# Three norms of a fp32 transformer block turned on VectorE through DRAM, a new opening, and an order by forward and backward passes

## The chip, the cores and the metric

The kernel runs on one core of a Trainium2 chip. The metric is device time in microseconds (us). Matmuls and PE transposes run on TensorE (PE, with its weight loads shown as PEld), elementwise work on VectorE (DVE) and ScalarE (ACT), a few memsets on GpSimd (POOL). SyncE (SP) only issues DMAs; they run on 16 DMA engines shared by all queues. Each engine takes its instructions in a fixed order and waits at the first one whose inputs are not there.

## The reference

A pre-norm block on x of 2048 rows by 640 columns in fp32: windowed attention (32 heads of 20, a window of 8 keys two rows apart), then a SwiGLU feed-forward of 1728. The norms have no weights.

```python
def _layernorm(x, eps=1e-5):
    return (x - mean(x)) / sqrt(var(x) + eps)

qkv = _layernorm(x) @ wqkv                 # 640 x 1920
idx = pos[:, None] - arange(8) * 2         # negative ones are masked
o = softmax(q . k[idx] * Dh**-0.5) . v[idx]
h = x + o @ wo                             # 640 x 640
n = _layernorm(h)
out = h + (silu(n @ w_gate) * (n @ w_up)) @ w_down
```

## The kernel before, in words

The 2048 rows are four blocks (`NB`, called blocks 0 to 3 here, numbered b) of 512; a block is four row groups j of 128 rows (`NJ`). Columns go in five chunks of 128 (`NC`), heads in four groups g of 8 (`NG`), the feed-forward in 13 tiles of 128 columns and a last one of 64 (`NF`).

**Products in three passes.** Every fp32 operand of a product is split into a high half, rounded to PE's fp32r type by an ACT cast, and a low half, the rest, made by a DVE subtraction. A product is hi·hi + lo·hi + hi·lo in three PE passes. So each operand costs PE nothing before its product, but ACT a cast and DVE a subtraction.

**PE's work.** The qkv products are L415: 15 matmuls of 480 columns for a (b, g, j), 64 such groups. The output product of attention is L586, 480 matmuls of 320 columns. Gate and up are L649, three passes of five matmuls for each of two banks (5 and 6), 1620 in all; down is L665, into banks 0 to 4, 820 in all. Before qkv and before gate/up the normed rows have to stand turned, columns on partitions. In `x_columns`, five groups of four 128x128 PE transposes (L316, `to_columns`) turn a block into a bank; ACT casts it (L319) and DVE subtracts (L320). Block 0's first norm is turned in the opening row group by row group (L376, casts L378, subtractions L379). `warm` (L331) issues matmuls on zeros ahead of the first data. `finish` turns the fifth 128 columns of the down product back (L707), adds on DVE (L714, L718) and stores (L722).

**The norms.** `LnStats.one` is the ACT form: a pass that sums the rows (L258, an Identity whose output nobody needs), the negated mean (L259), for ln1 a pass that centres (L261) and one that squares and sums (L266). `one_dve` does the same with BN statistics on DVE (L276 to L278); in the opening row groups j = 0, 1, 2 use it and j = 3 uses ACT. `rstd` has a square root on ACT and a Newton step on DVE (L289 to L293); `apply` (L306) scales. For ln2 of block 3 alone (`TURN = (3,)`), `apply` writes the rows in columns of 32 instead, DVE transposes 32x32 pieces of the whole tile (L738), four DMAs write it to the scratch `xsc` in DRAM (L740), one reads it back turned (L744), and ACT and DVE split it into shb (L733, L734). No PE transposes are needed there.

**Loads.** x of block 0 is loaded by row groups (L348), qkv weights a chunk at a time (L388, cast L389, subtraction L391), five chunks for a head group. A constant of 160 columns holds the attention mask and the identity matrix that the PE transposes use (L751). Tiles of feed-forward weights come by L623, are cast by L624 and L625 and split by L641; block 0 stores the low halves to the scratch `lsc`, and blocks 1 and 2 read them back (L629) instead of computing them. Attention goes through DRAM scratch as well; its DVE products are L463 and L468 (q·k) and L494 to L502 (weights times v, one multiply for each row group, then a tree of adds).

**The order.** The program records operations with an engine, a cost, the tiles they read and write, and a priority. `Plan.order` runs a list scheduler over them, whose start times set the order on every engine and in the queue of SP; semaphores follow from reads and writes. So any change of operations or costs moves the order elsewhere too.

Of the kernel before, what the change touches and what calls it, by code (L numbers as in the profile page):

```python
# [1 line left out]

# [8 lines left out]
F32 = mybir.dt.float32  # L11
# [12 lines left out]
NF = 14  # L24
KEPT = range(NF)
LOADED = (1, 2)
TURN = (3,)
# [8 lines left out]
class Plan:  # L36

# [20 lines left out]
    def order(self):  # L60
# [57 lines left out]
        self.end = max(free.values())  # L118
        self.start = start
        return sorted(range(len(ops)), key=lambda n: (start[n], n))  # L120
# [17 lines left out]
def program(tc, x_in, wqkv_in, wo_in, ffn_in, ffl_in, const_in, out):  # L138
# [4 lines left out]
    FA_N = 16320 + 128 + 640 + 2688  # L143
    RA_N = 19200

    with tc.tile_pool(name="sb", bufs=1) as sb, tc.tile_pool(
# [26 lines left out]

        banks = [psp.tile([128, 512], F32, name=f"bank{i}") for i in range(8)]
# [5 lines left out]
        xsc = dr.tile([NB, D, 4, 128], F32, name="xsc")  # L180
        lsc = dr.tile([NF, 128, 1920], F32, name="lsc")

# [7 lines left out]
        KV = carve(3 * 1760)  # L190
        QT = carve(2 * 640)
        PROD = carve(2560)
        OG = carve(640)
        XN = carve(4 * 640)
        LG = carve(2 * 256)
        MX = carve(2 * 64)
# [22 lines left out]

        ident = f(IDENT, 128)  # L220
# [4 lines left out]
        P.add("DVE", 0.8, lambda: V.memset(f(PROD, 1120), 0.0), w=[rf(PROD, 1120)], prio=0)  # L225

        def zero_halo(t):
            Q.dma_start(
                t[:, :, 0 : W - 1, :].rearrange("g a r c -> (g a) (r c)"),
                fa[0 : NG * 2, PROD : PROD + 1120],  # L230
            )

        for nm, t in (("K", ksc), ("V", vsc)):
            P.add(
                "SP", 0.07, lambda t=t: zero_halo(t), r=[rf(PROD, 1120)],
# [4 lines left out]
        class LnStats:  # L240
# [11 lines left out]
            def one(self, j):  # L252
                src, xo = self.src, XN + 640 * j
                SUM, NEG, SS = self.SUM + j, self.NEG + j, self.SS + j
                junk = (lambda: act_t()[:, 3072:3712]) if self.turned else (lambda: f(xo, 640))

                def s1():
                    A.activation(junk(), src(j), AF.Identity, accum_out=f(SUM, 1))  # L258
                    A.mul(f(NEG, 1), f(SUM, 1), -1.0 / D)  # L259
                    if self.center:  # L260
# [3 lines left out]
                P.add("ACT", 1.95 if self.center else 2.15, s1, r=[self.srcr(j)], w=[("ab", 3072, 3712) if self.turned else rf(xo, 640), rf(SUM, 1), rf(NEG, 1)] + ([] if self.center else [rf(SS, 1)]), prio=self.prio)  # L264
                if self.center:
                    P.add("ACT", 1.0, lambda: A.activation(src(j), f(xo, 640), AF.Square, accum_out=f(SS, 1)),  # L266
                          r=[rf(xo, 640)], w=[self.srcr(j), rf(SS, 1)], prio=self.prio + 1)
# [13 lines left out]
            def rstd(self, j, n, after=()):  # L281
                STD, RS, TM, NEG, NB = (o + j for o in (self.STD, self.RS, self.TM, self.NEG, self.NB))
                var, vr, sc = f(self.SS + j, n), rf(self.SS + j, n), 1.0 / D
                if j in self.ondve:
                    var, vr, sc = f(MV + 2 * j + 1, 1), rf(MV + 2 * j, 2), 1.0
# [42 lines left out]
        def warm(n, after=()):  # L328
            def mm():
                for _ in range(n):  # L330
                    T.matmul(banks[4][:, 0:128], r_(WARM, 128), r_(WARM, 128), start=True, stop=True)  # L331
# [509 lines left out]
```

## Time and profile before

| | |
|---|---|
| median of 3 runs | 865.08 us (864.16 to 865.6) |
| span of the profiled execution | 863.4 us |
| PE transposes of norms, L316 | 120, 16.7 us busy |
| PE transposes of block 0's first norm, L376 | 20, 4.1 us |
| warm-up matmuls, L331 | 23, 5.4 us |
| DVE statistics, L276 | 6, 2.6 us |
| turning on DVE, L738 | 1, 2.8 us |
| PE clock granted | 1.00 in every stretch asked |

The span counts from the first to the last instruction of one execution; the time of a run has about 1.7 us (865.08 - 863.4) around it. "Busy" of PE counts a matmul until its last column has drained, so consecutive matmuls overlap: the step from one to the next, which a long chain row gives, is what a matmul costs, and not its mean duration. A row of the timeline shows start, duration of the whole run, engine, line, operation, count, and in brackets how long the engine was idle before it and who released it.

### The profile page before, as it was taken

To read this page: it belongs to the slowest core of one execution; us is meant where nothing else is said; L and a number is where in the kernel's file an instruction comes from. 1 tells how busy PE (TensorE), PEld (TensorE's weight loads), DVE (VectorE), ACT (ScalarE), POOL (GpSimd) and SP (SyncE) were. 2 spreads that over 40 slices of the span, in tenths; PEclk is the share of its full clock that TensorE was granted. 3 is DMA by queue.
4 is the path that set the end of the run, shared out by engine and by line. 5 is a ranking of instruction groups with operands and counts; after the bars stand their busy time and mean duration, and the time that the engine had idled before them with its cause. 6 is when DMAs were issued, how large, how long until landed. Compare 5 with 4: busy or idle time off the path is not lost.

```text
span 863.4 us, 10743 instructions
## 1 busy us (share of the span) xinstructions
PE 857.4 (99%) x4059; PEld 731.0 (85%) x4059; DVE 645.4 (75%) x743; ACT 402.4 (47%) x651; POOL 1.8 (0%) x8
## 2 busy tenths in 40 slices
PE   9999999999999999999999999999999999999998
PEld 8888888889888888988888898888898887888886
DVE  7499999999989999988989898999622226333332
ACT  6867743233753435564434457443447324332321
POOL 0000000000000000000000000000000000000000
PEclk9999999999999999999999999999999999999999
DMA  7997766497597978568997985897733755222301
GB/s 266 269 295 215 177 173 173 141 285 189 168 332 237 292 243 302 139 182 277 344 276 243 321 238 165 256 340 226 251 122 117 248 185 197 92 92 92 102 21 61
DMA packets 74611, 180.10 MB, mean 209 GB/s; under 512 B 28720, under 2 KB 39344, under 8 KB 73792
## 3 DMA queue, kind: packets, MB, share of 16 engines
q1 hardware_dynamic: 74560, 179.43, 66.7%
q8 instruction: 31, 0.51, 0.2%
q14 instruction: 20, 0.16, 0.1%
HBM read 138.36 MB, written 41.03 MB: 208 GB/s over the span
## 4 chain that ended last, share of the span: by engine, by line
PE 98%; DVE 1%; DMA 1%; ACT 0%; SPq 0%; issue 0%; DVEq 0%; ACTq 0%
PE bank L649 42%; PE bank L415 24%; PE bank L665 21%; PE bank L586 8%; PE bank L316 2%; DMA fa<-in_x_dram 1%; PE bank L376 0%; PE bank L707 0%; DVE ra L641 0%; ACT ra L624 0%; DVE fa L276 0%; DVE acts L694 0%; DVE fa L692 0%; DVE shb L734 0%; DVE fa L278 0%
## 5 line engine op out<-in xcount | busy, mean ns | idle before, releaser
L649 PE MATMUL bank<-shb,ra 128*128 128x512 f32 x1620 | 378.9, 389 | 0.0
L649 PEld LDWEIGHTS bank<-shb,ra 128*128 128x128 f32 x1620 | 303.3, 188 | 62.2 <-ACT fa L683 0.2
L665 PE MATMUL bank<-ra,acts 128*128 128x512 f32 x656 | 160.5, 391 | 0.0
L665 PEld LDWEIGHTS bank<-ra,acts 128*128 128x128 f32 x656 | 122.4, 188 | 25.1
L684 DVE TENSOR_TENSOR fa<-bank,fa 128x512 f32<-128x512 f32 x52 | 35.9, 690 | 119.0 <-PE bank L649 118.8
L415 PE MATMUL bank<-ra,sha 128*128 128x480 f32 x480 | 107.6, 383 | 0.0
L415 PE MATMUL bank<-ra,shb 128*128 128x480 f32 x470 | 104.9, 380 | 0.0
L415 PEld LDWEIGHTS bank<-ra,sha 128*128 128x128 f32 x480 | 90.7, 190 | 13.5
L415 PEld LDWEIGHTS bank<-ra,shb 128*128 128x128 f32 x470 | 87.4, 188 | 12.8
L624 ACT CAST ra<-fa 128x1280 fp32r<-128x1280 f32 (+1 forms) x56 | 68.8, 1228 | 62.5 <-PE bank L649 60.4
L494 DVE TENSOR_TENSOR fa<-fa 128x1280 f32<-128x1280 f32 x64 | 93.1, 1486 | 0.8
L502 DVE TENSOR_TENSOR fa<-fa 128x1280 f32<-128x1280 f32 (+2 forms) x96 | 89.8, 935 | 2.8
L463 DVE TENSOR_TENSOR fa<-fa 128x2560 f32<-128x2560 f32 x32 | 90.3, 2820 | 1.4 <-DMA fa<-qsc 1.0
L468 DVE TENSOR_REDUCE fa<-fa 128x128 f32<-128x2560 f32 x32 | 90.1, 2816 | 0.7
L683 ACT ACTIVATE fa<-bank 128x512 f32<-128x512 f32 x52 | 31.1, 599 | 108.5 <-PE bank L649 108.4
L641 DVE TENSOR_TENSOR ra<-fa,ra 128x640 fp32r<-128x640 f32 (+1 forms) x82 | 64.8, 818 | 17.5 <-ACT ra L625 15.0
L586 PE MATMUL bank<-ra 128*128 128x320 f32 x480 | 74.5, 309 | 0.0
L586 PEld LDWEIGHTS bank<-ra 128*128 128x128 f32 x480 | 72.4, 188 | 2.1
L420 ACT ACTIVATE st<-bank,fa 128x480 f32<-128x480 f32 x64 | 42.1, 661 | 68.4 <-PE bank L415 59.1
L625 ACT CAST ra<-fa 128x640 fp32r<-128x640 f32 x56 | 40.7, 729 | 64.7 <-PE bank L665 64.6
L685 ACT CAST acts<-fa 128x512 fp32r<-128x512 f32 x52 | 32.2, 619 | 41.0 <-DVE fa L684 40.9
L665 PE MATMUL bank<-acts,ra 128*128 128x512 f32 x164 | 46.4, 391 | 0.6 <-DVE acts L694 0.6
(85 smaller groups left out, 497.4 us busy)
## 6 DMA issues: line engine op xcount, KB each, us to landing
fa<-in_ffn_dram SPq DMA_DIRECT2D x52, 960.0 KB, 6.1
ra<-lsc SPq DMA_DIRECT2D x26, 640.0 KB, 5.6
fa<-ksc SPq DMA_DIRECT2D x32, 440.0 KB, 5.8
fa<-vsc SPq DMA_DIRECT2D x32, 440.0 KB, 6.7
ra<-lsc SPq DMA_DIRECT2D x30, 320.0 KB, 3.2
lsc<-ra SPq DMA_DIRECT2D x13, 640.0 KB, 6.4
ksc<-st SPq DMA_DIRECT2D x32, 160.0 KB, 3.7
qsc<-st SPq DMA_DIRECT2D x16, 320.0 KB, 3.5
```

Source lines behind the costliest of these rows:

```text
L415: T.matmul(banks[bk][:, 0:480], l, r_(wq(g, w, c), 480), start=(p, c) == first_mm, stop=(p, c) == last_mm)
L420: P.add("ACT", act(480) + 0.06, lambda bk=bk, j=j: A.activation(stage_t()[:, so : so + 1920].rearrange("p (t j c) -> p t j c", t=3, j=NJ)[ ...
L463: P.add("DVE", dve(2560), lambda: V.tensor_tensor(f(PROD, 2560).rearrange("p (j w c) -> p j w c", j=2, w=W), window(ko, 2 * jp), f(qo + 32 ...
L468: P.add("DVE", dve(2560), lambda: V.tensor_reduce(f(lo + 128 * jp, 128), f(PROD, 2560).rearrange("p (n d) -> p n d", d=DH), axis=AX.X, op= ...
L494: V.tensor_tensor(f(PROD + 1280 * jj, 1280).rearrange("p (w h d) -> p w h d", w=W, d=DH), f(vo + 160 * j, 1280).rearrange("p (w h d) -> p ...
L502: V.tensor_add(dst(v), v[:, :, 0:m, :], v[:, :, m : 2 * m, :])
L586: T.matmul(banks[bk][:, 0:320], l, r_(m, 320), start=p == 0 and c == 0, stop=p == 2 and c == NC - 1)
L624: P.add("ACT", act(n), lambda: A.copy(r_(gu, n), f(raw, n)), r=[rf(raw, n)], w=[rr(gu, n)], prio=PR["fh"])
L625: P.add("ACT", act(640), lambda: A.copy(r_(dn[0], 640), f(raw + n, 640)), r=[rf(raw + n, 640)], w=[rr(dn[0], 640)], prio=PR["fh"])
L641: P.add(eng, c, lambda o=o: E.tensor_sub(ra[p0:, lo + o : lo + o + 640], fa[p0:, raw + o : raw + o + 640], ra[p0:, hi + o : hi + o + 640]. ...
L649: T.matmul(banks[bk], r_(gu + 1280 * w + wid * c + col, 128), x2(a, c), start=p == 0 and c == 0, stop=p == 2 and c == NC - 1)
L665: T.matmul(banks[k], l, m, start=first and p == 0, stop=last and p == len(passes) - 1)
```

## The change

**Turned norms.** `TURN = (3,)` becomes `TURN1, TURN2 = (2,), (2, 3)`. Ln1 and ln2 of block 2 now also go the way of block 3's ln2. `ln2_turn` becomes `turn` with a second scratch `ysc`, and `turned_columns` serves both. In the turned ln1 the summing pass writes the output that nobody needs onto its own source rows, and the centred rows go to `XN` in columns of 32. Wherever ln2 is not turned (block 1 now too), `rstd` and `apply` take three row groups first, then the last one; turned ones take all four at once.

**The opening.** Warm-up goes from 20 matmuls of 128 columns to 10 of 512, and from 3 between the first row groups to one of 512. The identity is made on GpSimd, and only the mask is loaded, later. SP issues x0, weights chunk 0, x1, chunks 1 and 2, chunks 3 and 4, x2, x3; before it was x0, the constant, x1, the five chunks, x2 and x3. Later weights also come two chunks to a DMA. Row groups j = 2 and 3 take ACT statistics, and `rstd` takes two groups at once.

**Attention.** K, V, q and products have tiles of their own, and the two multiplies by v of 1280 columns become one of 2560 (64 instructions become 32).

**The order.** The list scheduler (`listed`) gives start times; then all operations are placed from the end backwards and from the start forwards by modelled durations and latencies, twice; then 35 seeded moves (`MOVES`) shift some start times at random and repeat the passes. The final sequence is the sort by start.

```diff
-TURN = (3,)
+TURN1, TURN2 = (2,), (2,3)
...
+MOVES = [
+    (1000023, 3, 0.01), (1000040, 3, 0.01), (1000200, 3, 0.05), (1000252, 3, 0.01), (1001109, 3, 0.01), (1001162, 1, 0.05), (1001237, 1, 0.05), (1001256, 1, 0.01),
...
+    def forward(self, key):
+        st, lanes = [0.0] * len(self.ops), {}
+        for n in self.sort(key):
+            t = max([st[d] + self.dur[d] + self.gap(d, n) for d in self.pred[n]], default=0.0)
+            st[n] = lanes.setdefault(self.ops[n][0], Lane()).early(t, self.dur[n])
+        return st
+
+    def backward(self, st):
+        ends = [s + d for s, d in zip(st, self.dur)]
...
+    def move(self, st, seed, spread, share):
+        r = random.Random(seed)
+        key = [s + (r.gauss(0, spread) if r.random() < share else 0.0) for s in st]
+        return self.forward(self.backward(self.forward(key)))
+
+    def order(self):
+        st = self.listed()
+        self.model()
+        for _ in range(2):
+            st = self.forward(self.backward(st))
+        for m in MOVES:
+            st = self.move(st, *m)
+        return self.sort(st)
...
-                junk = (lambda: act_t()[:, 3072:3712]) if self.turned else (lambda: f(xo, 640))
+                away = self.turned and not self.center
+                junk = (lambda: act_t()[:, 3072:3712]) if away else (lambda: src(j)) if self.turned else (lambda: f(xo, 640))
...
-                    if self.center:
+                    if self.center and self.turned:
+                        A.activation(f(XN, 2560).rearrange("p (f j t) -> p f j t", j=NJ, t=32)[:, :, j, :], src(j).rearrange("p (f t) -> p f t", t=32), AF.Identity, bias=f(NEG, 1))
+                    elif self.center:
...
-        def warm(n, after=()):
+        def warm(n, wide, after=()):
...
+        def turned_columns(t, nm, prio):
...
+            src = lambda k: f(XN + 512 * k, 512).rearrange("p (q j t) -> p j q t", q=4, j=NJ)
...
+            for k in range(NC):
+                col = lambda a, k=k: t()[:, 2560 * a : 2560 * a + 2560].rearrange("p (j c q t) -> p c j q t", j=NJ, c=NC, q=4)[:, k]
+                P.add("ACT", act(512), lambda col=col, k=k: A.copy(col(0), src(k)), r=[rf(XN + 512 * k, 512)], w=hiv(k), prio=prio)
+                P.add("DVE", dve(512), lambda col=col, k=k: V.tensor_sub(col(1), src(k), col(0).bitcast(F32)),
+                      r=[rf(XN + 512 * k, 512), *hiv(k)], w=lov(k), prio=prio)
+
+        def turn(nm, dst, prio, first=False):
+            P.add("DVE", dve(2560), lambda: V.transpose(f(XN, 2560), f(XN, 2560)), r=[rf(XN, 2560)], w=[rf(XN, 2560)], prio=prio)
+            for q in range(4):
+                P.add("SP", 0.65, lambda q=q: Q.dma_start(
...
+            P.add("SP", 0.65, lambda: Q.dma_start(f(XN, 2560).rearrange("p (k t) -> p k t", k=NC), dst.rearrange("(k c) q t -> c k (q t)", c=128)),
...
+                if b in TURN1:
+                    turn(f"Y{b}", ysc[b], PR["ln1"], True)
+                    turned_columns(t, nm, PR["t1"])
+                    return
...
-                    warm(3, [("b5", 0, 0.25)])
-                (st.one_dve if j < 3 else st.one)(j)
+                    warm(1, 512, [("b5", 0, 0.25)])
+                (st.one_dve if j < 2 else st.one)(j)
...
-            for j in range(NJ):
-                st.rstd(j, 1, [(nm, 3200 + 1280 * (j // 2), 3840 + 1280 * (j // 2))])
...
+            for j in (0, 2):
+                st.rstd(j, 2, [(nm, 3200 + 640 * j, 3840 + 640 * j)])
+
+        def load_wqkv(g, parts=((0, 1), (2, 3), (4,))):
+            for ks in parts:
...
-                if b == 0 and j >= NJ - 2:
+                if b not in TURN2 and j >= NJ - 2:
...
-            if b:
+            if b in TURN2:
...
-        warm(20)
-        P.add("SP", 0.45, lambda: Q.dma_start(f(MASK, 160), const_in), w=[rf(MASK, 160)], prio=0, nbytes=nb(128, 640))
+        warm(10, 512)
+
+        def eye():
+            G.memset(ident, 1.0)
+            G.affine_select(ident, ident, pattern=[[-1, 128]], compare_op=ALU.is_equal, fill=0.0, base=0, channel_multiplier=1)
+        P.add("POOL", 1.2, eye, w=[rf(IDENT, 128)], prio=0)
+        load_wqkv(0, ((0,),))
         load_x(0, (1,))
-        load_wqkv(0)
+        load_wqkv(0, ((1, 2), (3, 4)))
         load_x(0, (2, 3))
```

**Where the order moves.** In these rows a name ahead of the arrow is what is written. In the change L810 is gate/up, L826 down, L868 the turning back in `finish`, L575 qkv, L444 the PE transposes of norms, L549 the casts of qkv weights, L532 the casts of block 0's turned rows, and L382, L383, L387 are the sum, the negated mean and the centring on ACT.

First place: ACT in the opening, before,

```order
L389 CAST ra_66<-fa_65 128x480
L378 CAST sha_133<-bank7_75 128x512
L378 CAST sha_133<-bank5_73 128x128
L389 CAST ra_66<-fa_65 128x480
L378 CAST sha_133<-bank6_74 128x512
L378 CAST sha_133<-bank5_73 128x128
L389 CAST ra_66<-fa_65 128x480 x3
L296 ACTIVATE fa_65<-fa_65 128x1 x2
L258 ACTIVATE fa_65<-fa_65 128x640
L259 ACTIVATE fa_65<-fa_65 128x1
L261 ACTIVATE fa_65<-fa_65 128x640
```

and in the change:

```order
L532 CAST sha_122<-bank5_73 128x128
L532 CAST sha_122<-bank7_75 128x512
L549 CAST ra_66<-fa_65 128x480 x2
L532 CAST sha_122<-bank6_74 128x512
L549 CAST ra_66<-fa_65 128x480 x2
L382 ACTIVATE fa_65<-fa_65 128x640
L383 ACTIVATE fa_65<-fa_65 128x1
L387 ACTIVATE fa_65<-fa_65 128x640
L382 ACTIVATE fa_65<-fa_65 128x640
L383 ACTIVATE fa_65<-fa_65 128x1
L387 ACTIVATE fa_65<-fa_65 128x640
L532 CAST sha_122<-bank5_73 128x128
```

The cast of the second row group's last chunk (bank 5) moves from ahead of the centring passes to behind both of them.

Second place: PE at the first feed-forward tile of block 0 (banks 5 and 6 of L649, then L810), before,

```order
L316 MATMUL bank6_74<-fa_65 128x128 x4
L316 MATMUL bank5_73<-fa_65 128x128 x4
L316 MATMUL bank7_75<-fa_65 128x128 x4
L415 MATMUL bank2_70<-ra_66,shb_67 128x480 x15
L316 MATMUL bank6_74<-fa_65 128x128 x4
L415 MATMUL bank3_71<-ra_66 128x480 x5
L415 MATMUL bank3_71<-ra_66,shb_67 128x480 x5
L415 MATMUL bank3_71<-ra_66 128x480 x5
L649 MATMUL bank5_73<-shb_67,ra_66 128x512 x5
L649 MATMUL bank6_74<-shb_67,ra_66 128x512 x5
```

and in the change:

```order
L444 MATMUL bank6_74<-fa_65 128x128 x4
L444 MATMUL bank5_73<-fa_65 128x128 x4
L444 MATMUL bank7_75<-fa_65 128x128 x4
L575 MATMUL bank3_71<-ra_66 128x480 x5
L575 MATMUL bank3_71<-ra_66,shb_67 128x480 x5
L575 MATMUL bank3_71<-ra_66 128x480 x5
L444 MATMUL bank6_74<-fa_65 128x128 x4
L810 MATMUL bank5_73<-shb_67,ra_66 128x512 x5
L810 MATMUL bank6_74<-shb_67,ra_66 128x512 x5
```

The last group of transposes moves from ahead of the last 15 qkv matmuls to directly ahead of gate/up, which reads what it turns.

Third place: the end on PE (down products into banks 0 to 4), before,

```order
L665 MATMUL bank4_72<-acts_2090,ra_66 128x512 x5
L665 MATMUL bank0_68<-ra_66,acts_2090 128x512 x5
L707 MATMUL bank4_72<-fa_65 128x128 x4
L665 MATMUL bank1_69<-ra_66,acts_2090 128x512 x5
L665 MATMUL bank2_70<-ra_66,acts_2090 128x512 x5
L665 MATMUL bank3_71<-ra_66,acts_2090 128x512 x5
```

and in the change:

```order
L826 MATMUL bank3_71<-ra_66,acts_1997 128x512 x8
L826 MATMUL bank4_72<-acts_1997,ra_66 128x512 x5
L826 MATMUL bank1_69<-ra_66,acts_1997 128x512 x5
L868 MATMUL bank4_72<-fa_65 128x128 x4
L826 MATMUL bank0_68<-ra_66,acts_1997 128x512 x3
L826 MATMUL bank2_70<-ra_66,acts_1997 128x512 x5
L826 MATMUL bank0_68<-ra_66,acts_1997 128x512 x5
```

Bank 0 is finished last instead of bank 3; only row group 3, which bank 3 feeds, is added and stored in two pieces at the end of the last block.

More of the change, by code (lines that the diff above doesn't have):

```diff
@@ L58, in add, with listed @@
         return n
-    def order(self):
+    def listed(self):
         ops = self.ops
@@ new lines, in sort @@
+    def sort(self, key, back=False):
+        pre, post, sg = (self.succ, self.pred, -1) if back else (self.pred, self.succ, 1)
+        left = [len(p) for p in pre]
+        h = [(sg * key[n], sg * n) for n in range(len(left)) if not left[n]]
+        heapq.heapify(h)
+        out = []
+        while h:
+            n = sg * heapq.heappop(h)[1]
+            out.append(n)
+            for m in post[n]:
+                left[m] -= 1
+                if not left[m]:
+                    heapq.heappush(h, (sg * key[m], sg * m))
+        return out
```

235 lines of the change are left out of this document (150 added, 85 removed), and 4 rows, old and new, of the table MOVES.

## The prediction

> **What bounds the kernel now.** I read the page first, then PE's own waits, then the chain of waits and PE's timeline where the change touches it. From the page: the span, the busy times of the engines, and the shares of the chain that ended last.
>
> ```profile
> span 863.4 us, 10743 instructions
> PE 857.4 (99%) x4059; PEld 731.0 (85%) x4059; DVE 645.4 (75%) x743; ACT 402.4 (47%) x651; POOL 1.8 (0%) x8
> PE 98%; DVE 1%; DMA 1%; ACT 0%; SPq 0%; issue 0%; DVEq 0%; ACTq 0%
> ```
>
> PE is busy 99% of the span and carries 98% of the chain. That leaves 6 us in which it does nothing. The list of PE's waits names 2.1 of them:
>
> ```profile
> PE bank L331 <- POOL ra L748: 1.0, 1, 1.0
> PE bank L665 <- DVE acts L694: 0.6, 1, 0.6
> PE bank L376 <- DVE fa L278: 0.5, 1, 0.5
> ```
>
> No wait in the middle of the program is for a transposed norm, an attention product or a load. So PE's work sets the time, and a change pays only by taking instructions off PE, by letting them run at the full step in the opening, or by shortening the two ends. The full step is read from long unbroken rows of the chain (start, duration, line, count):
>
> ```profile
> 118.85 74.53 PE bank L415 x345
> 580.42 6.80 PE bank L649 x30
> ```
>
> 74.53 / 345 = 0.216 us for a qkv matmul, 6.80 / 30 = 0.2267 us for one of the feed-forward.
>
> **The change part by part.** *The turned norms.* Two norms of block 2 lose five groups of four PE transposes each. What they cost is the distance to the next row, not their busy time. From PE's timeline, at ln1 of block 2 and then at ln2 of block 2:
>
> ```profile
> 65.60 1.03 PE L316 MATMUL bank<-fa 128*128 128x128 f32 x8
> 66.39 3.50 PE L415 MATMUL bank<-ra,shb 128*128 128x480 f32 x15
> 69.72 0.60 PE L316 MATMUL bank<-fa 128*128 128x128 f32 x4
> 70.08 3.50 PE L415 MATMUL bank<-ra,shb 128*128 128x480 f32 x15
> ...
> 558.42 1.47 PE L316 MATMUL bank<-fa 128*128 128x128 f32 x12
> 559.65 0.95 PE L665 MATMUL bank<-ra,acts 128*128 128x512 f32 x3
> ```
>
> Eight take 0.79 us (66.39 - 65.60), four 0.36, twelve 1.23. The 15 qkv matmuls between take 3.33 us (69.72 - 66.39) where 15 x 0.216 = 3.24, so each return to other work costs 0.09 more. Ln1 goes in lots of 8, 4 and 8: 0.79 + 0.36 + 0.79 + 3 x 0.09 = 2.2 us. Ln2 goes in lots of 4, 4 and 12: 0.36 + 0.36 + 1.23 + 3 x 0.09 = 2.2. Together **-4.4 us**, and nothing of it was hidden, since PE waited for nothing there.
>
> What takes their place lies on other engines. The rows of the one norm that is turned so already, with an attention multiply of each kind:
>
> ```profile
> L738 DVE STREAM_TRANSPOSE fa<-fa 128x2560 f32<-128x2560 f32 x1 | 2.8, 2845 | 0.1
> xsc<-fa SPq DMA_DIRECT2D x4, 320.0 KB, 6.4
> fa<-xsc SPq DMA_DIRECT2D x1, 1280.0 KB, 7.0
> L494 DVE TENSOR_TENSOR fa<-fa 128x1280 f32<-128x1280 f32 x64 | 93.1, 1486 | 0.8
> L463 DVE TENSOR_TENSOR fa<-fa 128x2560 f32<-128x2560 f32 x32 | 90.3, 2820 | 1.4 <-DMA fa<-qsc 1.0
> 50.00:100.00 50.00, 50.00 (x248) 43.55 (x248) 48.88 (x47) 34.72 (x69) 0.00 (x0) 1.00 0.80 228
> ```
>
> DVE gets 2 x 2.85 us more for the turning, and loses 32 x (2 x 1.486 - 2.82) = 4.9 us where two multiplies of 1280 become one of 2560 (taking the price of L463 for it), so its sum hardly moves. That matters because the last row, a stretch of 50 us by engine (PE, PEld, DVE, ACT, POOL, then clock, DMA share and GB/s), has DVE busy 48.88 of 50: it has no room there, but PE waits for it nowhere. The chain of a turned norm is 2.85 + 6.4 + 7.0 us for turning, writing and reading, some 16 us more than transposes on PE, before the same casts. For ln2 of block 2 the order puts some 180 feed-forward matmuls (41 us) between the last output product and the first gate/up that reads it; ln1 of block 2 has over 60 us of qkv products ahead. Block 3's turned norm in before has no row in the list of waits. I cost both chains at nothing; without that cover each would cost up to its 16 us. The summing pass that now writes onto its source rows has the length it had, and only the later squaring writes there too: nothing.
>
> *The opening.* PE's timeline up to the first transposes of block 1; the four rows in the middle are from narrow windows, one record of two matmuls each:
>
> ```profile
> 1.00 4.53 PE L331 MATMUL bank<-ra 128*128 128x128 f32 x20 [1.00 <-POOL ra L748]
> 8.87 5.96 PE L415 MATMUL bank<-ra,sha 128*128 128x480 f32 x20
> 15.14 1.13 PE L415 MATMUL bank<-ra,sha 128*128 128x480 f32 x4
> 16.57 14.54 PE L415 MATMUL bank<-ra,sha 128*128 128x480 f32 x66
> 30.95 0.60 PE L316 MATMUL bank<-fa 128*128 128x128 f32 x4
> ...
> 9.82 1.00 PE L415 MATMUL bank<-ra,sha 128*128 128x480 f32 x2
> 10.22 1.00 PE L415 MATMUL bank<-ra,sha 128*128 128x480 f32 x2
> ...
> 12.08 0.60 PE L415 MATMUL bank<-ra,sha 128*128 128x480 f32 x2
> 12.52 0.59 PE L415 MATMUL bank<-ra,sha 128*128 128x480 f32 x2
> ```
>
> The first 20 qkv matmuls take 5.96 us, 0.29 each against 0.216: 1.5 us lost. Their step is 0.40 us at 9.82 (10.22 - 9.82) and 0.44 for two, 0.22 each, at 12.08, while the column of the granted clock says 1.00 throughout. So PE runs at about half rate until some 11 us, in spite of the warm-up from 1.00 on. The warm-up is now 10 matmuls four times as wide. The most that a full step from the start can bring is those 1.5 us, plus the 0.5 of the wait for L278, if weights that are ahead of x1 in the queue let PE start before it: 2.0. Against it stands ACT's new order:
>
> ```profile
> 9.75 1.58 ACT L389 CAST ra<-fa 128x480 fp32r<-128x480 f32 x3
> 11.61 0.72 ACT L258 ACTIVATE fa<-fa 128x640 f32<-128x640 f32 x1
> 12.69 0.83 ACT L261 ACTIVATE fa<-fa 128x640 f32<-128x640 f32 x1
> ```
>
> One sum and centring takes 1.91 us (11.61 to 13.52); two of them now stand ahead of the cast of x1's last chunk, which so comes not before 14.4, where it came at 9.8. Its matmuls are the last of the first 30, behind it the low half on DVE. At a full step from 8.4 PE would be there at about 14.5, so it waits there and gives back some of the 2.0; at half rate it arrives later and waits less, but keeps the 1.5. I bound the gain by 0.25 and 2.0 and take **-1.0**, the middle.
>
> On this the Trainium skill, "TensorE: Matmul & The Clock Gate", Part 1: The HAM clock gate, says that the array runs at half clock until about 3.4 us of sustained activity, whatever the number of matmuls. The trace does not agree for this warm-up: 4.53 us of narrow ones from 1.00 on were followed by steps of 0.40 us some four microseconds after they ended. It would agree if narrow ones on zeros count for little or the pause from 5.5 to 8.9 was too empty.
>
> *The tail of block 2.* The wait of 0.6 us for L694 is behind this row of ACT, in the same stretch:
>
> ```profile
> 714.64 1.66 ACT L733 CAST shb<-fa 128x512 fp32r<-128x512 f32 x3
> ```
>
> Three casts of turned columns stood between the last tile's silu and its cast. In the change one stands there, 0.55 instead of 1.66 us: **-0.6**, at worst 0.
>
> *The first gate/up of block 0.* The order puts the last group of PE transposes directly ahead of L810; before, 15 qkv matmuls (3.2 us) covered its cast. The price is that of an earlier group, PE and ACT:
>
> ```profile
> 233.50 0.60 PE L316 MATMUL bank<-fa 128*128 128x128 f32 x4
> 234.25 0.56 ACT L319 CAST shb<-bank 128x512 fp32r<-128x512 f32 x1
> ```
>
> The cast ends at 234.81, 1.31 after the transposes began; 0.36 of it PE works. So PE waits about **+0.9**; 0.4 if ACT is free at once, 1.8 if another cast stands ahead. The low half is not read until the third pass.
>
> *The end.* After the last matmul, before adds two halves and stores 128 KB; the change adds 512 columns and stores 320 KB. The last adds, then the landing of stores and of loads of x:
>
> ```profile
> 859.65 0.76 DVE L714 TENSOR_TENSOR h<-bank,h 128x256 f32<-128x256 f32 x2 [0.44 <-PE bank L665]
> ...
> DMA to landing us min/median/max: 2.2/6.9/8.7
> ...
> DMA to landing us min/median/max: 2.9/6.0/6.3
> ...
> DMA to landing us min/median/max: 2.7/4.2/9.7
> ```
>
> The first landing row is the stores (L722), the second the x loads of 320 KB (L348), the third the low halves read back (L629, for later). The add costs the same (one of 512 against two of 256). The store: 2.9 for 320 KB on an idle queue against 2.2, **+0.7**; 0 if size does not count, 4.7 at the median of 6.9, against which speaks that nothing else moves then.
>
> Sum: 863.4 - 4.4 - 1.0 - 0.6 + 0.9 + 0.7 = 859.0 us of span. The median of the runs is 1.7 above this profiled span (865.08 - 863.4), so the time is **860.7 us**. Its own range: with 2.0, 0.4 and 0 for opening, first gate/up and end it is 858.5, with 0.25, 1.8 and 0.7 it is 862.4.
>
> **The rivals.** *A: the clock is up early.* If the wide warm-up brings full steps from the first real matmul and ACT's order holds PE little, the opening gives 1.65 instead of 1.0 and the time is 860.0. [...] By the Trainium skill's rule of 3.4 us on that page this is what happens. Against: the narrow ones did not do it.
>
> *B: the opening gives nothing but 0.25.* Half rate stays and the late cast of x1 takes the rest: 861.4. For it: ACT's row of 1.91 twice. Against: half rate ends some 3 us after the start in before too.
>
> *C: DVE in order.* The new order may put an attention multiply of 2.82 us ahead of the product that empties bank 6 (L684 in before). The product's row:
>
> ```profile
> L684 DVE TENSOR_TENSOR fa<-bank,fa 128x512 f32<-128x512 f32 x52 | 35.9, 690 | 119.0 <-PE bank L649 118.8
> ```
>
> The next gate/up into that bank comes 15 matmuls later, 15 x 0.2267 = 3.4 us. The multiply, 2.82, the product, 0.69, a silu of the same size ahead of it and the handing over make some 4.8 (an estimate from these rows), so a place costs 1.4. Three such places cost 4.2: 864.9, no change. For it: DVE busy 98%. Against: in before the same multiply stood in the same queue and there is no such wait.
>
> *D: slower, by late loads.* In the change the buffer of the low half of the last down weights (320 KB, read back) comes free 26 matmuls, 5.9 us, before its product at the end of block 1, and 31, 7.0 us, at the end of block 2; in before no load of this kind had under 12.5 us. At the landing of 9.7 with 0.3 us to issue, PE waits 10.0 - 5.9 = 4.1 and 10.0 - 7.0 = 3.0, and the time is 867.8. It decides from a landing of 8.4 at both (then 4.4 us are given back, the whole gain), and from 9.2 measurably. For it: the maximum of the row of L629. Against: its median is 4.2.
>
> **How the numbers follow.** Forecast 0.42, A 0.18, B 0.14, C 0.12, D 0.14. What differs by less than 0.2% (1.7 us) cannot be told from no change in a measurement of this kernel. So forecast, A and B, all under 863.35, are faster, with 0.02 of C: 0.76. Same: most of C and the edge of D, 0.10. Slower: 0.14. The predicted time is the forecast's. The range runs from its low end, 858.5, to 865.0, so that it holds C; D is left out. Among the faster cases alone it is 858.5 to 862.4.
>
> **What would show it right or wrong.** Right: 80 records of the norms' transposes instead of 120 and no PE wait for shb or the qkv operands of block 2; the first 90 qkv matmuls done at about 30.0 instead of 30.95; no wait of down for the last tile's low half; a new wait of 0.9 at the first gate/up near 243 us; a last store that lands 2.9 us after its issue. Wrong: PE waits for turned columns of block 2 (cover too short), rows of PE waiting for a DVE product before gate/up (C), or for DMA before the last down of blocks 1 and 2 (D), or a half-rate step lasting beyond 12 us (B).

## The result, and the profile after

The changed kernel takes 859.23 us (median of 4 runs, 858.89 to 859.39), the kernel before 865.34 us (4 runs, 864.16 to 867.15). The ratio is 0.9925, with a 95% interval of 0.9908 to 0.9942. (Now and then one execution runs at a lower granted clock: of eleven runs of a variant below, one took 1063.96 us at 0.75 and is left out of its range.) The profiled execution spans 857.1 us where it was 863.4: 6.3 us less. From the page of the changed kernel:

```profile
span 857.1 us, 10563 instructions
PE 850.7 (99%) x4007; PEld 723.4 (84%) x4007; DVE 643.5 (75%) x705; ACT 405.7 (47%) x658; POOL 2.5 (0%) x10
PE 98%; DMA 1%; SPq 0%; ACT 0%; DVE 0%; issue 0%
```

PE still carries 98% of the chain. It has 52 instructions fewer (40 transposes and 12 warm-ups), and DVE's busy time has hardly moved (645.4 before). PE's waits:

```profile
PE bank L459 <- POOL ra L892: 1.4, 1, 1.4
PE bank L530 <- DVE fa L406: 0.5, 1, 0.5
PE bank L810 <- ACT shb L447: 0.4, 1, 0.4
PE bank L575 <- ACT ra L549: 0.2, 1, 0.2
```

The 0.6 us for the last tile's low half is gone, and a wait of 0.4 ahead of gate/up is new. No row waits for a turned column (L486, L487), for an attention product or for a load.

PE's timeline in the opening and at the first gate/up of block 0:

```profile
1.38 4.63 PE L459 MATMUL bank<-ra 128*128 128x512 f32 x10 [1.38 <-POOL ra L892]
5.82 0.78 PE L530 MATMUL bank<-fa 128*128 128x128 f32 x5
...
8.53 4.27 PE L575 MATMUL bank<-ra,sha 128*128 128x480 f32 x18 [0.23 <-ACT ra L549]
...
14.95 17.55 PE L575 MATMUL bank<-ra,sha 128*128 128x480 f32 x80
32.34 0.60 PE L444 MATMUL bank<-fa 128*128 128x128 f32 x4
...
240.90 0.60 PE L444 MATMUL bank<-fa 128*128 128x128 f32 x4
241.25 0.48 PE L810 MATMUL bank<-shb,ra 128*128 128x512 f32 x1
242.17 3.01 PE L810 MATMUL bank<-shb,ra 128*128 128x512 f32 x12 [0.44 <-ACT shb L447]
...
850.03 3.24 PE L826 MATMUL bank<-ra,acts 128*128 128x512 f32 x13
```

And the rows of before that stand against them, with the wait for L694:

```profile
5.49 1.33 PE L376 MATMUL bank<-fa 128*128 128x128 f32 x5
...
714.30 2.88 PE L665 MATMUL bank<-ra,acts 128*128 128x512 f32 x12
717.81 0.73 PE L665 MATMUL bank<-acts,ra 128*128 128x512 f32 x2 [0.63 <-DVE acts L694]
...
855.91 3.70 PE L665 MATMUL bank<-ra,acts 128*128 128x512 f32 x15
```

105 qkv matmuls are done at 32.34; 15 of them take 15 x 0.216 = 3.24, so the 90th is done at 29.10, where it was at 30.95: 1.85 us gained. The five transposes at 5.82 take 0.78 us, those of before at 5.49 took 1.33, so in this execution PE runs at its full step before 6 us. At gate/up the second matmul comes 0.92 us after the first instead of 0.23: the wait of 0.44 costs 0.69 us of steps. The last matmul ends at 853.27 (before: 859.61), and from there to the end of the span it is 3.8 us in both.

So the 6.3 us are 1.85 from the opening, 0.79 from the wait for L694 (12 matmuls, 2.72 us at the full step, took 3.51 in before, from 714.30 to 717.81), 4.4 from the two norms, and 0.69 given back at gate/up: 6.35. Three of these are read from the rows; the 4.4 is the prediction's own sum, which closes the account and is tried by itself below.

### The profile page after: what moved, and what is told of

It is laid out like the page before. It is cut to its first block, busy times and chain, and to the rows that moved or that the text cites. A ratio compares the mean times of both kernels' runs of the same rounds, so it can differ in the third digit from the quotient of the medians.

```text
span 857.1 us, 10563 instructions
## 1 busy us (share of the span) xinstructions
PE 850.7 (99%) x4007; PEld 723.4 (84%) x4007; DVE 643.5 (75%) x705; ACT 405.7 (47%) x658; POOL 2.5 (0%) x10
## 4 chain that ended last, share of the span: by engine, by line
PE 98%; DMA 1%; SPq 0%; ACT 0%; DVE 0%; issue 0%
PE bank L810 43%; PE bank L575 24%; PE bank L826 22%; PE bank L747 8%; PE bank L444 1%; DMA fa<-in_wqkv_dram 1%; PE bank L868 0%; PE bank L530 0%; SPq L476 0%; DVE h L875 0%; ACT ra L549 0%; ACT shb L447 0%; SPq L546 0%
## 5 line engine op out<-in xcount | busy, mean ns | idle before, releaser
L810 PE MATMUL bank<-shb,ra 128*128 128x512 f32 x1620 | 386.7, 390 | 0.4 <-ACT shb L447 0.4
L810 PEld LDWEIGHTS bank<-shb,ra 128*128 128x128 f32 x1620 | 303.4, 188 | 62.9 <-ACT shb L447 0.8
L826 PE MATMUL bank<-ra,acts 128*128 128x512 f32 x656 | 167.1, 391 | 0.0
L826 PEld LDWEIGHTS bank<-ra,acts 128*128 128x128 f32 x656 | 122.5, 188 | 24.7
L845 DVE TENSOR_TENSOR fa<-bank,fa 128x512 f32<-128x512 f32 x52 | 35.8, 689 | 107.4 <-PE bank L810 92.0
L575 PE MATMUL bank<-ra,sha 128*128 128x480 f32 x480 | 107.0, 381 | 0.2 <-ACT ra L549 0.2
L575 PE MATMUL bank<-ra,shb 128*128 128x480 f32 x470 | 103.0, 379 | 0.0
L575 PEld LDWEIGHTS bank<-ra,sha 128*128 128x128 f32 x480 | 89.4, 188 | 13.7 <-ACT ra L549 0.5
L575 PEld LDWEIGHTS bank<-ra,shb 128*128 128x128 f32 x470 | 88.1, 188 | 13.1
L663 DVE TENSOR_TENSOR pq<-pq 128x1280 f32<-128x1280 f32 (+2 forms) x96 | 89.7, 934 | 2.4
L623 DVE TENSOR_TENSOR pq<-kv,pq 128x2560 f32<-128x2560 f32 x32 | 90.3, 2822 | 0.9 <-DMA kv<-ksc 0.4
L654 DVE TENSOR_TENSOR pq<-kv,pq 128x2560 f32<-128x2560 f32 x32 | 90.3, 2822 | 0.7
L628 DVE TENSOR_REDUCE pq<-pq 128x128 f32<-128x2560 f32 x32 | 90.0, 2813 | 0.4
L844 ACT ACTIVATE fa<-bank 128x512 f32<-128x512 f32 x52 | 31.1, 598 | 94.1 <-PE bank L810 89.3
L826 PE MATMUL bank<-acts,ra 128*128 128x512 f32 x164 | 46.1, 390 | 0.0
```

The lines of the kernel that those rows point to most:

```text
L575: T.matmul(banks[bk][:, 0:480], l, r_(wq(g, w, c), 480), start=(p, c) == first_mm, stop=(p, c) == last_mm)
L623: P.add("DVE", dve(2560), lambda: V.tensor_tensor(pq(PROD, 2560).rearrange("p (j w c) -> p j w c", j=2, w=W), window(ko, 2 * jp), pq(qo + ...
L628: P.add("DVE", dve(2560), lambda: V.tensor_reduce(pq(lo + 128 * jp, 128), pq(PROD, 2560).rearrange("p (n d) -> p n d", d=DH), axis=AX.X, o ...
L654: V.tensor_tensor(pq(PROD, 2560).rearrange("p (j n d) -> p j n d", j=2, d=DH), bass.AP(tensor=v.tensor, offset=v.offset, ap=[list(v.ap[0]) ...
L663: V.tensor_add(dst(v), v[:, :, 0:m, :], v[:, :, m : 2 * m, :])
L810: T.matmul(banks[bk], r_(gu + 1280 * w + wid * c + col, 128), x2(a, c), start=p == 0 and c == 0, stop=p == 2 and c == NC - 1)
```

## Experiments

The warm-up, the price of a PE transpose, the new wait and the order were tried apart; then more norms were turned. Each time stands beside 859.23 of the change, unless another partner is named.

**Narrow warm-up.**

```diff
-                for _ in range(n):
-                    T.matmul(banks[4][:, 0:wide], r_(WARM, 128), r_(WARM, wide), start=True, stop=True)
+                for _ in range(20 if n == 10 else 3):
+                    T.matmul(banks[4][:, 0:128], r_(WARM, 128), r_(WARM, 128), start=True, stop=True)
```

> The changed kernel with the warm-up of before: 20 matmuls of 128 columns (and 3 between the first row groups) in place of 10 of 512 (and 1), in the same place of the same order. Theory: the opening's gain of 1.85 us (90th qkv matmul done at 29.10 instead of 30.95) comes mostly from full-rate steps from the first real matmul, which the wide warm-up brings. Then the first qkv matmuls step at about 0.40 us again until some 3 us after they start, the 90th is done at 30.2 to 30.6, and the time is 860.3 to 860.7, 1.1 to 1.5 us above the changed kernel. Rival: the gain comes from the new order of loads and casts; then the 90th is done at 29.1 to 29.3 and the time is 859.2 to 859.4.

**Half as many wide ones**: `range(5 if n == 10 else 1)` in the same loop, wide as in the change.

> The changed kernel with 5 wide warm-up matmuls instead of 10, about 2.3 us instead of 4.63, in the same order. Theory: what releases the full rate is a stretch of dense work; the Trainium skill, TensorE: Matmul & The Clock Gate, Part 1, names some 3.4 us of it. In rows of this case: 4.63 us of wide matmuls were enough for full steps at 8.53; 2.3 us then are too few, the first qkv matmuls step at about 0.40 us, the 90th is done 1.0 to 1.5 us later than 29.10 and the time is 860.2 to 860.7. Rival: any wide matmuls ahead do, and the time stays at 859.2.

Measured: 860.38 us (5 runs, 859.07 to 861.97) and 860.39 us (859.31 to 860.69), each about 1.15 above the change. One run of each five (859.07 and 859.31) is as fast as the change; the profiles are of others, so what PE did in these two is open. PE's timeline of the narrow one (the profiled execution is its slowest, with a wait of 0.9 for L845 besides, far behind the opening):

```profile
1.39 4.53 PE L459 MATMUL bank<-ra 128*128 128x128 f32 x20 [1.39 <-POOL ra L892]
5.78 1.30 PE L530 MATMUL bank<-fa 128*128 128x128 f32 x5
...
8.35 5.44 PE L575 MATMUL bank<-ra,sha 128*128 128x480 f32 x19
...
33.33 0.60 PE L444 MATMUL bank<-fa 128*128 128x128 f32 x4
```

And of the short one:

```profile
1.38 2.50 PE L459 MATMUL bank<-ra 128*128 128x512 f32 x5 [1.38 <-POOL ra L892]
5.66 1.30 PE L530 MATMUL bank<-fa 128*128 128x128 f32 x5 [1.77 <-DVE fa L406]
...
8.18 5.51 PE L575 MATMUL bank<-ra,sha 128*128 128x480 f32 x19
...
33.24 0.60 PE L444 MATMUL bank<-fa 128*128 128x128 f32 x4
```

Both have transposes at half rate again (1.30), and the 105 matmuls are done 0.99 and 0.90 us later than at 32.34. Narrow windows of the timeline give the steps: 0.40 us up to about 10.5 in both, then 0.21 to 0.23. In the change they are 0.21 to 0.23 from 8.85 on, but for one of 0.32. So the width and the length of the warm-up are worth about 1.0 of the 1.85 us. The other 0.85 stay without them: with the narrow warm-up the first qkv matmul starts at 8.35 instead of 8.87 (0.52), without the wait of 0.5 for L278, and the half rate ends two matmuls earlier (the rest). Which of the changes in the opening, loads, identity or statistics, brought these was not tried apart. The rivals (time unchanged) fall.

Twenty narrow matmuls last as long as ten wide ones, 4.53 against 4.63 us. But a wide one steps by 0.43 us for 512 columns, and a narrow one by 0.21 for 128, where a quarter of 0.43 is 0.11: by this estimate columns stream through the array only half of the time with narrow ones. All three warm-ups are on zeros, so zeros are not the difference. Nor is a pause: in the narrow run PE has no named wait from 1.39 to 8.35 us, 7.0 us of narrow matmuls and transposes, and still steps by 0.40 afterwards. Eleven profiles here have the ten wide ones. In all of them the second group of five transposes, which begins at 7.1 to 8.4 us, steps by 0.11; the first group, from 5.6 to 5.8, still begins at 0.21 in five of them, so 6 us is the figure of this one execution. The Trainium skill, "TensorE: Matmul & The Clock Gate", Part 1: The HAM clock gate, asks for some 3.4 us of sustained activity. 4.63 us of wide ones were enough and 2.50 were not, which agrees; 4.53 us of narrow ones were not either, so here it was not the time alone, as the Trainium skill puts it there. That the share of time in which columns stream decides is the reading that fits these three; no run varied that share by itself.

**Every PE transpose of the other norms twice.**

```diff
-                for q in range(4):
+                for q in (0, 1, 2, 3, 0, 1, 2, 3):
                     T.transpose(banks[bk][:, 128 * q : 128 * q + 128], src(4 * u + q), ident)
```

> The changed kernel with the four remaining turned-on-PE norms issuing each of their 80 transposes twice, in the same order. It measures the disputed price by itself. Theory: a PE transpose costs its distance to the next row, 0.09 us (0.36 for four, 0.79 for eight), and none of it is hidden: 80 x 0.09 = 7.2 us more, time 866.2 to 866.8, PE idle unchanged to 0.3 us. So 40 of them are 3.6 us, the rest of the 4.4 forecast for the two norms being restarts (0.55). Rival: part of what PE does there is hidden behind casts and attention, or a transpose costs its busy share only: under 5 us more (time under 864.2).

Measured: 868.12 us (868.01 to 868.34), 8.89 above the change. The group's busy time, first of the change and then with doubling:

```profile
L444 PE MATMUL bank<-fa 128*128 128x128 f32 x80 | 11.0, 273 | 0.0
```

```profile
L444 PE MATMUL bank<-fa 128*128 128x128 f32 x160 | 19.7, 273 | 0.0
```

8.89 / 80 = 0.111 us for a transpose, more than the 0.09 expected. A lot of four takes 0.36 and loses 0.09 on the return to other work, and (0.36 + 0.09) / 4 is 0.11 as well; in a longer lot each costs 0.11 by itself (24 took 2.54 us). So there is no separate price of a restart, and 40 transposes are 40 x 0.111 = 4.4 us. That confirms the sum of the prediction, by another split. It is the price on PE alone; what the norms are worth with the chains that replace them is tried below.

**Both norms back on PE, with all moves.** `TURN1, TURN2 = (), (3,)`.

> The changed kernel with both norms of block 2 back on PE transposes (40 more of them); the opening, attention tiles and ordering passes stay. Theory: the two norms are worth 4.4 us, all of it PE work that nothing hid: time 863.3 to 863.9. Rival: part of the 6 us comes from the ordering passes and moves, and the turned chains cost something; then undoing them costs under 3 us (time under 862.2). A third: the ordering's moves fit only the changed operations, and without them new waits come: above 864.5.

Measured: 868.59 us (868.4 to 869.04), 9.4 above the change and above the kernel before too (ratio 1.0041, 1.0029 to 1.0054). The third way is what happened: PE's waits show it.

```profile
PE bank L810 <- ACT fa L844: 1.2, 2, 0.9
PE bank L810 <- DVE fa L845: 0.6, 2, 0.4
```

Silu and its product (L844, L845) hold gate/up, where the change has no such row. The moves draw random numbers operation by operation, so with other operations they move other ones. This run therefore doesn't price the norms.

**The order apart from the operations.** The same operations as in the change with the list scheduler's order, and with the passes but without the moves:

```diff
         st = self.listed()
-        self.model()
-        for _ in range(2):
-            st = self.forward(self.backward(st))
-        for m in MOVES:
-            st = self.move(st, *m)
-        return self.sort(st)
+        return sorted(range(len(st)), key=lambda n: (st[n], n))
```

> The changed kernel with the order of the list scheduler alone, no backward and forward passes and no moves; all operations as in the change. Theory: PE has the same work, and what the passes and moves are worth is waits alone. In the run with both norms back on PE the moves fitted nothing and some 5.0 us of lost steps appeared in the tails of blocks 0 and 1 and the first gate/up; the list order of before had 2.1 us of waits in all. So 1 to 4 us more than the change: 860.2 to 863.2. Rival: the list scheduler does not see how long the turned chains take and puts their readers too early; then each chain shows with up to its 16 us, 870 or more.

> The changed kernel with the passes and without the 35 moves. Theory: the moves were fitted to waits that the passes leave; without them 1 to 5 us come back, 860.2 to 864.2, at the same places as in the run without the turned norms (first gate/up near 241, tails near 404 and 558). Rival: the passes alone do the ordering and the moves nothing that can be measured: 859.0 to 859.8.

Measured: the list order 875.45 us (871.96 to 876.83), 16.2 above the change; the passes without moves 859.30 us (859.18 to 860.78), the same as the change. In both the theory falls and the rival holds. PE's first waits with the list order:

```profile
PE bank L805 <- ACT shb L481: 7.6, 1, 7.6
PE bank L439 <- ACT fa L382: 3.6, 2, 1.9
```

L805 is gate/up there, L481 the cast of turned columns, L439 the PE transposes and L382 the centring of block 3's ln1. The queue of SP shows why, with the list order and then in the change (write and read of the scratch; L492 and L497 are the reads):

```profile
548.16 0.87 SPq L488 DMA_DIRECT2D xsc<-fa  x2
549.13 3.76 SPq L671 DMA_DIRECT2D osc<-pq  x4
552.93 0.99 SPq L488 DMA_DIRECT2D xsc<-fa  x2
557.59 1.74 SPq L671 DMA_DIRECT2D osc<-pq  x4
559.43 3.16 SPq L785 DMA_DIRECT2D ra<-lsc  x4
562.65 0.43 SPq L492 DMA_DIRECT2D fa<-xsc  x1
```

```profile
530.69 4.04 SPq L493 DMA_DIRECT2D xsc<-fa  x4
...
539.19 0.37 SPq L497 DMA_DIRECT2D fa<-xsc  x1
```

The list order splits the four writes around other stores and issues the read at 562.65, behind loads that wait for their buffers. PE is ready for the columns at 564.80, 2 us later; in the change the read goes out 17.6 us ahead of gate/up at 556.83. It lands at 571.09, and the casts begin at 571.92, behind a softmax step on ACT (L636). The second wait is another cost of the turned ln1: the sums and the centring of block 3's ln1 go through the tile XN too, and ACT waits 4.46 us until block 2's columns have left it.

After the long wait PE is not at its full step at once. The granted clock is the third number from the end of these windows:

```profile
574.00:576.00 2.00, 2.00 (x5) 1.44 (x5) 2.00 (x5) 0.60 (x2) 0.00 (x0) 0.50 0.99 415
576.00:578.00 2.00, 2.00 (x8) 1.54 (x8) 0.52 (x1) 0.73 (x1) 0.00 (x0) 0.71 1.03 425
578.00:580.00 2.00, 2.00 (x10) 1.67 (x9) 0.00 (x0) 0.17 (x1) 0.00 (x0) 1.00 1.09 369
```

So a wait of 7.6 us costs more than 7.6: matmuls of 512 columns step by 0.43 at 576 us, as in the warm-up. The passes bring the turning forward to where its reader needs it. What makes this change pay is thus the backward and forward passes; the moves add nothing that can be measured.

**Both norms back on PE, passes without moves.** The fair partner is 859.30.

> Both norms of block 2 back on PE transposes, ordered by the passes without the moves, to be compared with the changed kernel without the moves (859.3). Theory: the 5 us above the 4.4 of the first run without the turned norms came from moves that fit other operations; the passes by themselves leave 0.6 us of waits either way. Then only PE's 40 transposes come back: 863.3 to 864.4. Rival: the passes place PE's transposes badly whatever the moves, and the turned norms are worth more than their PE work because they leave PE's order without places to wait: 866 or more.

Measured: 862.42 us (862.18 to 863.12), 3.1 more (3.8 by the spans of the profiled executions, 861.4 against 857.6; the 861.4 is of its slowest run). That is under the expected 4.0 to 5.1 and far from the rival. The turned kernel gives part of its 4.4 us back: between 520 and 560 us, ahead of block 2's first gate/up, the matmuls with turned norms take 1.0 us more than their full steps, those with PE transposes 0.2. The wait of 0.4 for L385, the centring, lies elsewhere, at 113, where the other run loses nearly as much. The fitted order of the change has the same time with other waits. Without the turned norms this kernel is still 2.5 us under the kernel before (864.90 beside it), which is about the 1.85 of the opening and the 0.79 of the wait for L694.

**The new wait ahead of gate/up.** First the last group of transposes was emitted earlier:

> The changed kernel with the last four PE transposes of block 0's second norm emitted five qkv matmuls earlier (after 10 of the last 15). Theory: the new wait ahead of the first gate/up (0.44 us idle, 0.69 us of lost steps) goes, since the cast then ends behind five qkv matmuls (1.08 us of cover plus what ACT is ahead): span 0.5 to 0.7 lower, 856.4 to 856.6, time 858.5 to 858.7. Rival: ACT is busy with evictions until 240.2, so the cast comes no earlier and the bank's low-half subtraction holds the transposes: span unchanged at 857.1 or later.

Measured: 859.97 us (859.86 to 860.43), span 858.1, no gain; the wait became two, 0.5 for the cast and 0.7 for L448. Pulling the group ahead in the program also put it ahead of subtractions of low halves that still had to read the bank. So those halves were taken from overwritten values, and they waited behind the new transposes. The second form delays the qkv matmuls instead and leaves the subtractions where they were:

```diff
+            if n == t:
+                mm(ps[:10])
+                P.ops[t][2]()
+                mm(ps[10:])
+            elif n != q:
+                P.ops[n][2]()
```

> The changed kernel with the last 15 qkv matmuls of the first phase split 10 and 5 around the last four PE transposes of block 0's second norm; every other engine keeps its order, and the low halves of the earlier columns stay ahead. Theory: the cast of that group then runs beside five qkv matmuls (1.08 us) and ends near 241.0, so the wait of 0.44 us (0.69 us of steps) ahead of the first gate/up goes: span 856.4 to 856.6, time 858.5 to 858.8. Rival: ACT's three evictions of qkv (until 240.2) or the low-half subtraction on DVE hold it, and the wait only changes its name: span 857.0 or more.

Measured: 858.56 us (858.2 to 859.21), span 856.3: 0.7 us less than the change, as expected, and the fastest of all. The ranges of the runs overlap, and against the kernel before the two ratios are alike (0.9924 and 0.9925), so the gain rests on the trace. PE's timeline there:

```profile
239.73 0.60 PE L444 MATMUL bank<-fa 128*128 128x128 f32 x4
240.08 1.32 PE L575 MATMUL bank<-ra 128*128 128x480 f32 x5
241.24 4.96 PE L810 MATMUL bank<-shb,ra 128*128 128x512 f32 x21
```

The 21 matmuls of gate/up run without a break behind five of qkv.

**More norms turned**, with the passes and no moves: `TURN2 = (1, 2, 3)`, then `TURN1 = (2, 3)`.

> The changed kernel without the moves, with ln2 of block 1 turned on DVE as well. Theory: 20 more transposes leave PE, 2.2 us, and the passes start the chain early enough: 856.8 to 857.5. Rival: in block 0's feed-forward DVE is full (98% busy from 50 to 560 us in before), the turning stands behind attention there, the read comes late as in the list order (7.6 us of wait at block 2's first gate/up), and it ends above 860.

> The changed kernel without the moves, with ln1 of block 3 turned as well. Theory of covers: its rows and those of ln1 of block 2 go through the same tile XN, which comes free only when block 2's columns are cast; the chain of 16 us and more for turning, writing and reading then stands between, and some 75 qkv matmuls (16 us) are the cover that block 2 leaves. So 0 to 8 us of new waits against 2.2 of PE work saved: 857 to 865, likeliest 861. Rival: the passes put other groups of qkv in between and it gives the full 2.2: 857.1.

Measured: 865.63 us (864.85 to 866.62) and 874.02 us (871.61 to 875.65), against 859.30. In the first the rival is what happened; in the second the theory's waits came and more. PE waits for turned columns in both (L484 cast, L485 subtraction). With ln2 of block 1, at its first gate/up, PE and then the read in SP's queue:

```profile
400.33 3.76 PE L808 MATMUL bank<-shb,ra 128*128 128x512 f32 x10 [0.71 <-ACT shb L484]
406.01 12.15 PE L808 MATMUL bank<-shb,ra 128*128 128x512 f32 x41 [1.92 <-DVE shb L485]
...
393.11 0.37 SPq L495 DMA_DIRECT2D fa<-xsc  x1
```

The read is issued 7 us ahead of its reader, in the change at block 2 it is some 18 (539.19 to 556.83). In the run with passes and no moves it is 11.4 (547.06 to 558.44), without a wait. The second wait here is not the read's: it landed at 399.64, and the subtractions (L485) begin at 405.27, behind attention and `finish` on DVE. With ln1 of block 3, PE and then ACT:

```profile
116.55 5.85 PE L573 MATMUL bank<-ra,shb 128*128 128x480 f32 x15 [4.35 <-ACT st L578]
136.17 3.52 PE L573 MATMUL bank<-ra,sha 128*128 128x480 f32 x15 [0.80 <-ACT st L578]
140.94 2.85 PE L573 MATMUL bank<-ra,shb 128*128 128x480 f32 x5 [1.26 <-ACT shb L484]
145.05 5.31 PE L573 MATMUL bank<-ra,shb 128*128 128x480 f32 x13 [1.26 <-DVE shb L485]
...
105.90 0.83 ACT L383 ACTIVATE fa<-fa 128x640 f32<-128x640 f32 x1 [8.20 <-DVE sha L485]
115.85 2.85 ACT L578 ACTIVATE st<-bank,fa 128x480 f32<-128x480 f32 x5
```

The last two rows of PE are the expected ones. The largest wait was not foreseen: an eviction of qkv on ACT (L578) holds a bank 4.35 us. It stands in ACT's order behind the centring, squaring and sums of block 3's ln1, from 105.90 to 115.5, and these wait 8.20 us until block 2's columns have left XN (L485). So it is the shared tile of the theory, at another place. Behind that wait, too, PE is at half step: the 15 matmuls at 116.55 take 5.68 us up to the next row at 122.23 where 15 x 0.216 = 3.24, and the granted clock there is 0.50. The loss is above the range expected.

**The unneeded output elsewhere.** The summing pass of the turned ln1 writes to `f(RAW + 640 * j, 640)` instead of its own rows. It overwrites raw weights there that were still to be read, so the weights differ; the work and the order are the same.

> The changed kernel with the unneeded output of the turned ln1's summing pass written to free columns of the raw weight tile instead of its own source rows; the order of every engine is the same. Theory: the pass takes the 0.73 us it takes elsewhere (0.73 for the sums of before), nothing waits for it, and the time is that of the change: 859.0 to 859.5, span 856.9 to 857.3. Rival: writing in place delays the centring that reads the same rows, and taking it away brings ln1 of block 2 forward: more than 0.5 us faster, or a shorter pass by over 0.05 us in the rows of ACT.

Measured: 859.22 us (858.78 to 859.74), span 856.8. The 14 summing passes of ln1, four of them of the turned one, have a median of 0.734 us there and 0.730 in the change. Where the output goes costs nothing.

## Why the prediction was right

Forecast were 860.7 us and a step of -4.4 against 865.08; measured were 859.23 and -6.1 against 865.34. By its steps:

- *The norms, -4.4.* Confirmed as PE's price: the doubled transposes give 0.111 us each, 4.4 for 40. The split into 0.09 and restarts was a reading of the same thing. With an order that both share, the two norms are worth 3.1 us (3.8 by the spans).
- *The chains, at nothing.* Confirmed in the change: no wait names a turned column. The reason given, a cover of 41 us of matmuls, is only half of it. With the list order the same operations wait 7.6 us, because the read is issued late. In the change the read of block 2's ln2 landed at 548.00, 8.8 us before PE read the columns at 556.83; the casts were placed late, from 553.69 to 556.39, and ended 0.44 us ahead of PE. The price of DVE was misread, without effect: 64 multiplies are 93.1 us busy and 32 double ones 90.3, so 2.8 us go and not 4.9.
- *The opening, -1.0.* Right mechanism, mis-sized: 1.85, near the upper bound of 2.0. About 1.0 is the step of the matmuls, which the warm-up sets, and 0.85 the rest of the opening. Taking the middle of the bounds was the step that failed; rival A had the mechanism (the wide warm-up brings the full step) and its 860.0 was nearer. The cast of x1's last chunk came at 13.99, as late as feared, but cost nothing: PE has no wait for it, since the transposes of the third row group and other qkv matmuls were ahead of it.
- *The wait for L694, -0.6.* It went, and its steps were worth 0.79.
- *The first gate/up, +0.9.* It came at the place named, 0.44 of idle and 0.69 of steps, and it goes when five qkv matmuls cover the cast.
- *The end, +0.7.* 0.0: from the last matmul to the end it is 3.8 us before and after, with a last store of 128 KB and of 320 KB. The 320 KB landed 2.1 us after the issue, not 2.9: the landing of a load of x at the start was the wrong measure of it.
- *Rivals.* C did not come: no wait for an eviction in the change, though one of that kind (L844, L845) comes when the moves fit nothing. D did not come: the reads at 549.32 and 704.78 (the latter 7.3 us ahead of its product) landed after 2.9 and 2.7 us, without a wait, and the row of landings of L790 has a median of 4.8, with a maximum of 14.7 where there was room. B fell, as the steps in the opening show.
- *The number.* The four mis-sized steps (0.85, 0.19, 0.21 and 0.7) all lean the same way and make the span 1.9 us shorter than the 859.0 forecast. The time is only 1.5 under, as the profiled run has 2.05 us around its span (859.15 - 857.1) and not 1.7.

## What to carry to other kernels

Where one engine carries 98% of the chain, count what a change takes off it by distances in its timeline, and check it by doubling the operation: 80 extra transposes priced one more exactly than undoing the change did. A way around through memory pays only if the order issues its transfers early enough and the tile on the way is free: the same operations took 16 us more with another order, and one more norm turned gave it all back. An ordering fitted to one set of operations prices nothing about another, so undo such a change with an order that both share.

## What the runs showed of the hardware

A warm-up of 20 matmuls of 128 columns left PE at half its step (0.40 us a qkv matmul until 10.5 us), one of ten of 512 columns and the same length had it at full step before 6 us in the change and by 8.6 us in all eleven profiles with it; five of 512 did not. In the opening the profile's column of the granted clock said 1.00 all the while, so the step between matmuls has to be read there. Behind waits in the middle it did tell: after 7.6 us of idle PE it said 0.50, with steps of 0.43 us for 512 columns, and after 4.35 us 0.50 as well, with 5.68 us for 15 qkv matmuls.

A last store of 320 KB ended no later after the last matmul than one of 128 KB.
